# A windowed-attention phase ahead of two expert layers: its instructions ordered by a list scheduler inside the kernel, with all PSUM banks in one pool

## The chip, the cores and the metric

One core of one Trainium2 chip runs the kernel. The engines are TensorE (PE, with its weight loads shown as PEld), VectorE (DVE), ScalarE (ACT), GpSimd (POOL) and the queue that issues most transfers (SP). The metric is the device time of one execution in microseconds (us).

## What is computed

Four batches of eight heads (512 local and 32 global tokens, 64 channels each) go through attention, and the result goes through two dense layers one after the other:

```python
s_g = scale * np.matmul(q_g, k_all.transpose(0, 1, 3, 2))
out_g = np.matmul(sm(s_g), v_all)
...
mask = np.abs(pos[:, None] - pos[None, :]) <= window
...
a_l = sm(s_l)
out_l = np.matmul(a_l, np.concatenate([v_g, v_l], axis=2))
...
return (silu * val @ w_out).astype(np.float32)
...
return (g @ w_out).astype(np.float32)
```

Local queries see the keys within 32 positions and the 32 global keys; global queries see all 544 keys. The first dense layer (512 to 1536 to 512) gates with silu, the second (512 to 2048 to 512) is a mish layer.

## The kernel before

**Two phases.** The first phase is the attention, in function `attention()` (L342). The second phase, from L644 on, holds the dense layers; it is emitted inside `tc.manual_schedule()`, that is, in the order written. The 2176 rows of x are cut in five column tiles of 512, 384, 384, 384 and 512 (`TILES`), x0 to x4; each value is kept as a high and a low part (x0h, x0l), and every dense product is three matmuls (high by high, high by low, low by high).

**A pair.** The attention works on pairs of heads: 4 batches of 4 pairs, 16 in all. `att_hp` (L197) takes one pair through its steps, each ended by a `yield`: turn queries and keys with 16 transposes (L195, tile qkT), copy them to SBUF (keys on DVE L211, queries on ACT L215, more keys on POOL L212 and L213); twice, for two halves, scores (L238, tile sc), masked minimum on DVE (L243) and exponential on ACT (L247); normalise on POOL (L228, L230); turn the weights (L195, tile pT) and copy them (ACT L265); multiply by the values (L272 and L276, tile o); split into x high (ACT L137) and x low (DVE L138). `att_g` (L281) does the same for the global queries of two pairs at once (tiles ga, gT, go), 8 times. `att_glob` (L325) prepares the global keys and queries of a batch.

**Fills.** The first group of the first dense layer is done early for x0, x1 and x2: `fill` (L524) emits, per tile, four accumulations of 12 matmuls (g and v, L538, for two slices of 128 hidden channels) and four of 6 (L559). They need x of a whole batch and the first six weight pieces. The weights are packed as doubles and are unpacked by `w_convert` (L399): a square on ACT (L407), four DVE operations (L409 to L413), a copy on ACT (L423) and a subtraction on POOL (L424).

**What sets the order.** `attention()` writes the steps down with hand-set times (pair n at 10n, converts at 16 to 48, fills at a priority of a million below), sorts them, and emits them in that order. The framework's scheduler then orders each engine's instructions itself, by priority and a timeline simulated at compile time (`schedule_with_timeline_sim=True`, L692). In the compiled program the steps of pairs, converts and fills stand interleaved.

**Buffers.** PSUM has 8 banks of 512 words per partition: three pairs of banks for the attention (`ps_pair`, `bank()` L143) and two single banks for the fills (`ps_mm`). Keys, queries, values and scores of a pair are double-buffered. SP issues the loads: six per pair for queries and keys (L162 to L166), four for values (L185 to L187), one per weight piece (L393, L396).

Of the kernel before, what the change touches and what calls it, by code (L numbers as in the profile page):

```python
# [21 lines left out]
def tile_attn_moe_moe2(  # L22
# [109 lines left out]
    def split_to_x(src, kd, nk, c0, n):  # L132
        for t, o, s, m in pieces(c0, n):
            xh, xl = x_tile(t)
            hi = xh[:, kd:kd + nk, o:o + m]
            lo = xl[:, kd:kd + nk, o:o + m]
            nc.scalar.activation(out=hi, in_=src[:, :, s:s + m], func=AF.Copy)  # L137
            nc.vector.tensor_tensor(out=lo, in0=src[:, :, s:s + m], in1=hi.bitcast(F32), op=ALU.subtract)  # L138
# [4 lines left out]
    def bank(name):  # L143

        return ps_pair.tile([128, 2, 512], F32, tag="pair", name=name)
# [3 lines left out]
    def load_glob(b):  # L149
        gk = g_p.tile([128, 2, 128], F32, tag="gkq", name="gkq")  # L150
        for i, src in enumerate((k_g, q_g)):
            for h in range(2):
                (nc.sync if b else nc.scalar).dma_start(out=gk[:, i, 64 * h:64 * h + 64],
                                  in_=src[b].rearrange("(g h) p d -> h g p d", h=2)[h])
        GK[b] = gk

    def load_qk(b, hp):
        hs = slice(2 * hp, 2 * hp + 2)
        qs = qk_p.tile([128, 4, 2, D], F32, tag="qs", name="qs")
        ks = qk_p.tile([128, 4, 2, D], F32, tag="ks", name="ks")  # L160
        for h in range(2):
            nc.sync.dma_start(out=ks[:, :, h], in_=k_l[b, 2 * hp + h].rearrange("(c p) d -> p c d", p=128))  # L162
            nc.sync.dma_start(out=qs[:, 0:3, h],
                              in_=q_l[b, 2 * hp + h, SG:SG + 384, :].rearrange("(c p) d -> p c d", p=128))
        nc.sync.dma_start(out=qs[0:96, 3], in_=q_l[b, hs, SG + 384:SL, :].rearrange("h p d -> p h d"))
        nc.sync.dma_start(out=qs[96:128, 3], in_=q_l[b, hs, 0:SG, :].rearrange("h p d -> p h d"))  # L166
        QS[b, hp], KS[b, hp] = qs, ks
# [29 lines left out]
    def att_hp(b, hp):  # L197


        qs, ks = QS.pop((b, hp)), KS.pop((b, hp))  # L200
        p = bank("qkT")
        for i, src in enumerate((ks, qs)):
            for r in range(4):
                for j in range(2):
                    transpose_half(p[:, j, 256 * i + 64 * r:256 * i + 64 * r + 64],
                                   src[half(j), r].rearrange("p h d -> p (h d)"), j)
        pk, pq = (p[:, :, 256 * i:256 * i + 256].rearrange("c j (r t) -> c r j t", t=64) for i in range(2))
        kst = kst_p.tile([128, 4, 224], F32, tag="kst", name="kst")
        KST[b, hp] = kst
        nc.gpsimd.tensor_copy(kst[:, :, 192:224], GK[b, "kT"][:, hp:hp + 1, :].to_broadcast([128, 4, SG]))  # L210
        nc.vector.tensor_copy(kst[:, :, 0:128].rearrange("c r (j t) -> c r j t", j=2), pk)  # L211
        nc.gpsimd.tensor_copy(kst[:, 0:3, 128:192], kst[:, 1:4, 0:64])  # L212
        nc.gpsimd.tensor_copy(kst[:, 3, 128:192], kst[:, 0, 0:64])  # L213
        qT = qk_p.tile([128, 4, 128], F32, tag="qT", name="qT")
        nc.scalar.activation(out=qT.rearrange("c r (j t) -> c r j t", j=2), in_=pq, func=AF.Copy)  # L215
        yield
        sm = sm_p.tile([128, NB, 224], F32, tag="sm", name="sm")
        sng = sm_p.tile([128, NB, SG], F32, tag="sng", name="sng")
        nb_ = st_p.tile([128, NB], F32, tag="nb", name="nb")
        su = st_p.tile([128, NB], F32, tag="su", name="su")  # L220
        rc = st_p.tile([128, NB], F32, tag="rc", name="rc")

        def normalise(g):
            i0, i1 = 4 * g, 4 * g + 4
            r = rc[:, i0:i1]
            nc.vector.tensor_scalar(r, su[:, i0:i1], 1e-9, None, op0=ALU.add)
            nc.vector.reciprocal(r, r)  # L227
            nc.gpsimd.tensor_tensor(out=sm[:, i0:i1, 0:192], in0=sm[:, i0:i1, 0:192],  # L228
                                    in1=r.unsqueeze(2).to_broadcast([128, 4, 192]), op=ALU.mult)
            nc.gpsimd.tensor_tensor(out=sng[:, i0:i1, :], in0=sm[:, i0:i1, 192:224],  # L230
                                    in1=r.unsqueeze(2).to_broadcast([128, 4, SG]), op=ALU.mult)


        for g in range(2):
            p = bank("sc")
            for pp in range(2):
                for h in range(2):
                    nc.tensor.matmul(p[:, h, 224 * pp:224 * pp + 224], lhsT=qT[half(h), 2 * g + pp, :],  # L238
                                     rhs=kst[half(h), 2 * g + pp, :], start=True, stop=True)
            for pp in range(2):  # L240
                for h in range(2):
                    i = 4 * g + 2 * pp + h
                    nc.vector.tensor_tensor_reduce(  # L243
                        out=sm[:, i], in0=p[:, h, 224 * pp:224 * pp + 224],
                        in1=mask7 if 2 * g + pp == 3 else mask, scale=-scale, scalar=3.0e38,
                        op0=ALU.add, op1=ALU.min, accum_out=nb_[:, i:i + 1])
                    nc.scalar.activation(out=sm[:, i], in_=sm[:, i], func=AF.Exp,  # L247
                                         bias=nb_[:, i:i + 1], scale=-1.0, accum_out=su[:, i:i + 1])
            if g:
                normalise(0)  # L250
            yield
        normalise(1)
        yield


        pt = []
        for g in range(2):
            p = bank("pT")
            for k in range(4):
                for j in range(2):  # L260
                    transpose_half(p[:, j, 64 * k:64 * k + 64], sm[half(j), 4 * g + k, 64 * j:64 * j + 128], j)
            for j in range(2):
                transpose_half(p[:, j, 256:320], sng[half(j), 4 * g:4 * g + 4].rearrange("q b x -> q (b x)"), j)
            pt.append(sm_p.tile([128, 2, 5, 64], F32, tag=f"pt{g}", bufs=1, name="pt"))
            nc.scalar.activation(out=pt[g].rearrange("k j x q -> k j (x q)"), in_=p[:, :, 0:320], func=AF.Copy)  # L265
            yield
        vw = VW[b, hp]
        p = bank("o")[:, 0]
        for r in range(4):
            for h in range(2):  # L270
                k = 2 * (r % 2) + h
                nc.tensor.matmul(p[half(h), 128 * r:128 * r + 128], lhsT=vg[:, k, hp, :],  # L272
                                 rhs=pt[r // 2][:, :, 4, :], start=(r == 0), stop=False)
        for i in range(NB):
            for h in range(2):
                nc.tensor.matmul(p[half(h), 64 * i:64 * i + 64], lhsT=vw[:, i, h, :],  # L276
                                 rhs=pt[i // 4][:, i % 2, 2 * (i // 2 % 2) + h, :], start=False, stop=(i == NB - 1))
# [418 lines left out]
```

## Time and profile before

| what | value |
|---|---|
| median of 3 runs | 1004.9 us (1004.61 to 1005.93) |
| profiled execution, its own time | 1006.5 us |
| span of that execution in the profile | 1004.8 us |
| PE busy over the span | 944.4 us (94%) |
| PE granted clock, mean | 0.973 of full speed |
| DVE, ACT, POOL busy | 571.8, 523.8, 362.0 us |

Times in the rows count from the start of the span. Busy time is time in which an engine has an instruction in flight; matmuls overlap one another, so the step from one group's start to the next group's start is shorter than the listed duration of a group. PEclk is the granted TensorE clock as a share of 2.4 GHz; 0.5 is the lower of its two levels. In the chain of waits each row is what held up the end at that moment.

### The profile page before, as it was taken

Reading aid. Unit: us, or ns where it says so; the run is one execution under the profiler, and the core shown is the slowest. Engines: PE = TensorE matmul, PEld = TensorE weight load, DVE = VectorE, ACT = ScalarE, POOL = GpSimd, SP = SyncE. Lnnn points to the kernel's source line nnn. Section 1 sums busy time; section 2 is a strip of 40 time slices with the busy share of each in tenths; the row PEclk is TensorE's granted clock in tenths of the full one; section 3 lists DMA queues with packets and bytes.
Section 4 is the critical chain, followed back from the end, with each engine's and each line's share of the span. In section 5 each row is a group of like instructions: output and inputs, shape, how many; then the busy total and the mean of one; then the engine's idle time right before and its main releaser. Section 6 shows DMA issues by size and latency. Waiting matters only on the chain.

```text
span 1004.8 us, 15751 instructions
## 1 busy us (share of the span) xinstructions
PE 944.4 (94%) x6008; PEld 822.3 (82%) x6008; DVE 571.8 (57%) x1097; ACT 523.8 (52%) x1058; POOL 362.0 (36%) x353
## 2 busy tenths in 40 slices
PE   5588987988999999999999999999999999999998
PEld 4366776767899899898898998898889789888986
DVE  3855554454888765846838745556444826562213
ACT  3456565554233222312223335788668867886664
POOL 3443343432443432323323454543234423342222
PEclk9688999987999999999999999999999999999999
DMA  6643343410222211201202101021102101100112
GB/s 141 192 109 75 90 93 85 94 43 22 78 70 84 63 64 36 69 22 42 76 10 63 63 1 43 22 63 43 42 22 64 63 22 42 43 22 1 59 47 73
DMA packets 101387, 59.21 MB, mean 59 GB/s; under 512 B 75072, under 2 KB 95552, under 8 KB 101312
## 3 DMA queue, kind: packets, MB, share of 16 engines
q1 hardware_dynamic: 100784, 58.08, 20.8%
q8 instruction: 47, 0.77, 0.3%
q14 instruction: 28, 0.23, 0.1%
q10 hardware_dynamic: 528, 0.13, 0.1%
HBM read 53.74 MB, written 4.46 MB: 58 GB/s over the span
## 4 chain that ended last, share of the span: by engine, by line
PE 80%; DVE 9%; ACT 7%; POOL 1%; issue 1%; DMA 1%; SPq 0%; DVEq 0%; ACTq 0%; POOLq 0%
PE acc L603 29%; PE h L447 16%; PE v L447 13%; PE g L447 13%; ACT sm L247 4%; PE sc L238 2%; DVE cx L412 1%; PE mm L559 1%; POOL sm L228 1%; PE g L538 1%; DVE fl L409 1%; PE v L538 1%; DVE sm L243 1%; PE pT L195 1%; DVE cx L411 1%
## 5 line engine op out<-in xcount | busy, mean ns | idle before, releaser
L458 POOL TENSOR_TENSOR al<-t,ah 128x384 fp32r<-128x384 f32 (+1 forms) x140 | 164.1, 1187 | 462.0 <-ACT ah L472 451.0
L472 ACT ACTIVATE ah<-t 128x384 fp32r<-128x384 f32 (+1 forms) x140 | 79.2, 566 | 147.2 <-DVE t L483 132.9
L512 DVE TENSOR_TENSOR t<-t,h 128x384 f32<-128x384 f32 (+1 forms) x80 | 47.1, 607 | 142.5 <-ACT t L511 142.3
L611 DVE TENSOR_TENSOR y<-acc,y 128x512 f32<-128x512 f32 (+1 forms) x151 | 92.6, 636 | 43.2 <-PE acc L603 42.5
L480 ACT ACTIVATE t<-g 128x384 f32<-128x384 f32 (+1 forms) x54 | 28.9, 536 | 134.0 <-PE g L447 133.0
L412 DVE SCALAR_TENSOR_TENSOR cx<-fl,cx 128x512 uint32<-128x512 uint32 x68 | 81.6, 1200 | 2.2
L228 POOL TENSOR_TENSOR sm<-sm,rc 128x768 f32<-128x768 f32 x32 | 47.5, 1484 | 91.3 <-DVE rc L227 78.6
L247 ACT ACTIVATE sm<-sm,nb 128x224 f32<-128x224 f32 x128 | 60.1, 471 | 35.6 <-DVE nb L243 35.5
L501 ACT ACTIVATE t<-h 128x384 f32<-128x384 f32 (+1 forms) x80 | 41.9, 523 | 58.3 <-PE h L447 58.2
L413 DVE SCALAR_TENSOR_TENSOR cx<-st,cx 128x512 uint32<-128x512 uint32 x68 | 67.2, 988 | 2.3
L481 DVE SCALAR_TENSOR_TENSOR t<-t,g 128x384 f32<-128x384 f32 (+1 forms) x54 | 32.7, 606 | 56.7 <-ACT t L480 56.6
L409 DVE SCALAR_TENSOR_TENSOR fl<-q,st 128x512 f32<-128x512 f32 x68 | 59.5, 875 | 9.6 <-ACT q L407 9.6
L483 DVE SCALAR_TENSOR_TENSOR t<-t,v 128x384 f32<-128x384 f32 (+1 forms) x54 | 32.9, 609 | 46.9 <-PE v L447 46.0
L243 DVE CUSTOM_DVE_ANT_0 sm<-sc,mask 128x224 f32<-128x224 f32 x128 | 42.2, 385 | 28.2 <-PE sc L238 28.2
L502 ACT ACTIVATE t<-t,cst 128x384 f32<-128x384 f32 (+1 forms) x80 | 52.8, 660 | 2.6
L511 ACT ACTIVATE t<-t,cst 128x384 f32<-128x384 f32 (+1 forms) x80 | 49.4, 649 | 0.3
L407 ACT ACTIVATE q<-st 128x512 f32<-128x512 f32 x68 | 44.6, 656 | 7.7 <-DMA st<-in_moe_w_gate 4.4
L411 DVE TENSOR_SCALAR cx<-fl 128x512 uint32<-128x512 uint32 x68 | 43.8, 644 | 5.6
L238 PE MATMUL sc<-kst,qT 64*128 64x224 f32 x256 | 38.7, 426 | 2.8 <-ACT qT L215 2.0
L511 ACT ACT_TABLE_LOAD x27 | 34.6, 1283 | 0.5
L500 ACT ACT_TABLE_LOAD x27 | 34.6, 1283 | 0.5
L195 PE MATMUL pT<-ident,sm 64*128 64x64 f32 x256 | 16.2, 252 | 18.9 <-POOL sm L228 18.3
(899 smaller groups left out, 2812.8 us busy)
## 6 DMA issues: line engine op xcount, KB each, us to landing
st<-in_moe_w_out SPq DMA_DIRECT2D x28, 512.0 KB
st<-in_moe_w_in SPq DMA_DIRECT2D x16, 512.0 KB
vw<-in_v_l SPq DMA_DIRECT2D x32, 224.0 KB
st<-in_moe_w_gate SPq DMA_DIRECT2D x12, 512.0 KB
st<-in_moe_w_val SPq DMA_DIRECT2D x12, 512.0 KB
ks<-in_k_l SPq DMA_DIRECT2D x32, 128.0 KB
qs<-in_q_l SPq DMA_DIRECT2D x32, 96.0 KB
out<-y SPq DMA_DIRECT2D x12, 256.0 KB
```

The lines of the kernel that those rows point to most:

```text
L228: nc.gpsimd.tensor_tensor(out=sm[:, i0:i1, 0:192], in0=sm[:, i0:i1, 0:192], in1=r.unsqueeze(2).to_broadcast([128, 4, 192]), op=ALU.mult)
L238: nc.tensor.matmul(p[:, h, 224 * pp:224 * pp + 224], lhsT=qT[half(h), 2 * g + pp, :], rhs=kst[half(h), 2 * g + pp, :], start=True, stop=True)
L247: nc.scalar.activation(out=sm[:, i], in_=sm[:, i], func=AF.Exp, bias=nb_[:, i:i + 1], scale=-1.0, accum_out=su[:, i:i + 1])
L409: nc.vector.scalar_tensor_tensor(fl, q, TINY2, hw, op0=ALU.is_ge, op1=ALU.mult)
L412: nc.vector.scalar_tensor_tensor(x, fu, 0xC0000000, x, op0=ALU.bitwise_and, op1=ALU.bitwise_or)
L413: nc.vector.scalar_tensor_tensor(x, st[:, :, 0], 29, x, op0=ALU.logical_shift_right, op1=ALU.bitwise_or)
L447: nc.tensor.matmul(p[:, 0:n], lhsT=a[:, d], rhs=c[:, k, :], start=(k == 0 and j == 0), stop=(k == KD - 1 and j == 2))
L458: nc.gpsimd.tensor_tensor(out=a[1][:, 0:n], in0=src, in1=a[0][:, 0:n].bitcast(F32), op=ALU.subtract)
L472: nc.scalar.activation(out=a[0][:, 0:n], in_=src, func=AF.Copy)
L511: nc.scalar.activation(out=s, in_=s, func=AF.Sin, scale=-2.0, bias=quarter)
L603: nc.tensor.matmul(p, lhsT=l, rhs=r, start=(first and j == 0), stop=(last and j == 2))
L611: nc.vector.tensor_tensor(out=ya, in0=p, in1=ya, op=ALU.add)
```

## The change

Each step of the attention, of the six weight conversions and of the three fills becomes a task: a name, a key (its nominal time), an engine, a duration, the tasks that it needs, the work that it emits, and the PSUM banks that it takes with the task that frees them. `in_order()` runs a list scheduler over the tasks while the kernel is built: whenever an engine is free it takes the task of lowest key whose needs are done and whose banks are free. The tasks are emitted in that order, now inside `tc.manual_schedule()`, so that each engine runs them as planned.

With it: the 8 PSUM banks are four fixed tiles of two banks, from which a task takes a pair (`both`) or one bank (`one`); the second phase gets its own `ps_mm` after the attention, and its PSUM pools wait tile by tile. A fill is cut into portions of three matmuls with keys above 1000. The conversions have keys from 35 on, 5 apart, and their four DVE operations are tasks of their own. The copy of the queries goes to ACT for even pairs and to DVE for odd ones. The scores of global queries against global keys (L289, two matmuls for each two pairs) are made once per batch in one bank (`GG`) and copied to SBUF. The loads are tasks of SP; the queries of pair 0 are issued from the ACT queue, and the first global keys and queries from SP instead of ACT.

The core of the diff (the work functions emit the instructions of before and are left out):

```diff
-    ps_mm = pool("ps_mm", 2, space=PS)
...
-    ps_pair = pool("ps_pair", 3, early, space=PS)
+    ps_pair = pool("ps_pair", 1, early, space=PS)
...
+    PAIR = [ps_pair.tile([128, 2, 512], F32, tag=f"pair{i}", name=f"pair{i}") for i in range(4)]
...
+    def both(task):
+        return PAIR[place[task][0] // 2]
+
+    def one(task):
+        i = place[task][0]
+        return PAIR[i // 2][:, i % 2]
...
+        eng = nc.sync if b or hp else nc.scalar
...
+        done, start, order = {}, {}, []
+        used = [None] * 8
+        free = {"PE": 0.0, "DVE": 2.0, "ACT": 2.5, "POOL": 3.0, "SP": 0.0}
+        wait = {e: sorted((n for n in tasks if tasks[n][1] == e), key=lambda n: tasks[n][0]) for e in free}
+        now = 0.0
+        while any(wait.values()):
+            for i in range(8):
+                if used[i] is not None and done.get(used[i], 1e9) <= now:
+                    used[i] = None
+            for e, queue in wait.items():
+                if free[e] > now:
+                    continue
+                for n in queue:
+                    key, _, room, needs, work, banks, until = tasks[n]
+                    if any(done.get(x, 1e9) > now for x in needs):
+                        continue
+                    if banks == 2:
+                        got = next(([2 * i, 2 * i + 1] for i in range(4) if used[2 * i] is used[2 * i + 1] is None), None)
+                    elif banks == 1:
+                        some = [i for i in range(8) if used[i] is None]
+                        got = [min(some, key=lambda i: used[i ^ 1] is None)] if some else None
+                    else:
+                        got = []
+                    if got is None:
+                        continue
+                    for i in got:
+                        used[i] = until
+                    place[n] = got
+                    late = {"PE": 0.25, "SP": 2.4}.get(e, 0.08)
+                    if n[0] == "w":
+                        late = 4.5
+                    free[e] = now + room
+                    done[n] = now + room + late
+                    order.append(n)
+                    queue.remove(n)
+                    break
+            later = [x for x in list(free.values()) + list(done.values()) if x > now]
+            if not later:
+                raise RuntimeError("no task can start: " + str({e: q[:3] for e, q in wait.items()}))
+            now = min(later)
+        return order
...
+        task(("A", n), t - 4, "PE", 0.65, [("qk", n)], qk, 2, ("Aq", n))
+        task(("Ag", n), t - 3.95, "POOL", 0.30, [("AGk", b), lastu("GA", n - 2), agog("S", 2, 1)], glob_keys)
+        task(("Ak", n), t - 3.9, "DVE", 0.69, [("A", n), lastu("GA", n - 2), agog("S", 2, 1)], keys)
+        task(("At", n), t - 3.8, "POOL", 0.55, [("Ak", n)], more_keys)
+        task(("Aq", n), t - 3.7, "ACT" if on_act else "DVE", 0.60 if on_act else 0.69,
+             [("A", n), ("Ak", n), agog("S", 2, 1)], queries)
...
+            task(("S", n, g), t + 0.5 * g, "PE", 0.98, [("Aq", n), ("At", n), ("Ag", n)], lambda g=g: scores(g), 2, ("M", n, g, 3))
+            for i in range(4):
+                task(("M", n, g, i), t + 0.5 * g + 0.1 * i, "DVE", 0.31,
+                     [("S", n, g), agog("C", 2, 1)], lambda g=g, i=i: minimum(g, i))
+                task(("E", n, g, i), t + 0.5 * g + 0.1 * i, "ACT", 0.49, [("M", n, g, i)], lambda g=g, i=i: exponential(g, i))
+            task(("R", n, g), t + 1 + g, "DVE", 0.38, [("E", n, g, 3)], lambda g=g: reciprocal(g))
+            task(("N", n, g), t + 1 + g, "POOL", 1.9, [("R", n, g), agog("C", 2, g)], lambda g=g: normalise(g))
+            task(("C", n, g), t + 2 + g, "PE", 0.42, [("N", n, g)], lambda g=g: turn(g), 2, ("V", n, g))
+            task(("V", n, g), t + 2 + g, "ACT", 0.70, [("C", n, g), ago("D", 1)], lambda g=g: turned(g))
...
+        task(("D", n), t + 4, "PE", 2.05, [("V", n, 0), ("V", n, 1), ("v", n), ("vg", b)], values, 1, ("Xl", n))
+        task(("Xh", n), t + 4, "ACT", 0.82 if b else 0.65, [("D", n)], lambda: x_high(src(), hp, 1, b * SL, SL))
+        task(("Xl", n), t + 4, "DVE", 0.90 if b else 0.70, [("Xh", n)], lambda: x_low(src(), hp, 1, b * SL, SL))
+        task(("qk", n), t - 24, "SP", 3.1 if n else 1.6, [ago("A", 2)], lambda: load_qk(b, hp))
+        task(("v", n), t - 12, "SP", 2.1, [ago("D", 2), lastu("GO", n - 2)], lambda: load_v(b, hp))
...
+        task(("GA", u), t, "PE", 0.95, [("Ak", n), ("Ak", n - 1), ("AGe", b)], scores, 1, ("GE", u))
+        task(("GM", u), t, "DVE", 1.1, [("GA", u), ("GGe", b)], minimum)
+        task(("GE", u), t, "ACT", 1.2, [("GM", u), ago("GT")], exponential)
+        task(("GR", u), t + 1, "DVE", 0.9, [("GE", u)], normalise)
+        task(("GT", u), t + 1, "PE", 0.40, [("GR", u)], turn, 2, ("GV", u))
+        task(("GV", u), t + 2, "ACT", 0.70, [("GT", u), ago("GO")], turned)
+        task(("GO", u), t + 3, "PE", 1.25, [("GV", u), ("v", n), ("v", n - 1), ("vgb", b)], values, 1, ("GXl", u))
...
+        task(("AGe", b), t + 3, "DVE", 0.6, [("AG", b, 1), ("AGk", b)] + prev(("GA", HP // 2 * b - 1), ("GG", b - 1)), queries)
+        task(("GG", b), t + 3, "PE", 0.3, [("AGe", b)], scores, 1, ("GGe", b))
+        task(("GGe", b), t + 3, "DVE", 0.2, [("GG", b)] + prev(("GE", HP // 2 * b - 1)), scored)
...
+        task(("Cq", i), t, "ACT", 0.67, [("w", i)] + ([("Cf", i - 1, 0)] if i else []), go)
+        for j, room in enumerate((0.7, 0.45, 0.68, 0.68)):
+            need = [("Cf", i, j - 1)] if j else [("Cq", i)] + ([("Cf", i - 1, 3), ("Cl", i - 2)][:i] if i else [])
+            task(("Cf", i, j), t + 0.1 * j, "DVE", room, need, go)
+        task(("Ch", i), t, "ACT", 0.63, [("Cf", i, 3)], go)
+        task(("Cl", i), t, "POOL", 1.3, [("Ch", i)], go)
...
+            add_pair(n)
+        for i in range(9):
+            task(("w", i), CT(i) - 10.0, "SP", 0.6, [("Cf", i - 3, 3)] if i > 2 else [], load_next)
+        for i in range(6):
+            add_convert(i)
+        for i in FILL:
+            add_fill(i)
+        for name in in_order():
+            tasks[name][4]()
...
+                    need = x_done + [("Cl", piece), before if c else None]
+                    task(("F", t, f, kind, c), key, "PE", 0.012 + n * 0.00142, need,
+                         lambda k=k, f=f, kind=kind, c=c: unit(k, f, kind, c),
+                         0 if c else 1, ("Fg" if kind == "g" else "Fp", t, f))
...
+                task(("F2", t, c, i), key, "PE", 0.012 + n * 0.00142, need, lambda c=c, i=i: second_part(c, i),
...
-    attention()
+    with tc.manual_schedule():
+        setup()
+        attention()
     early.close()
-    ps_acc = pool("ps_acc", 4, space=PS)
-    ps_at = pool("ps_at", 2, space=PS)
+    ps_acc = pool("ps_acc", 4, space=PS, reuse_waits="tile")
+    ps_mm = pool("ps_mm", 2, space=PS, reuse_waits="tile")
+    ps_at = pool("ps_at", 2, space=PS, reuse_waits="tile")
```

Names of tasks: A turns queries and keys; Ag, Ak, At, Aq copy them; S scores; M minimum; E exponential; R reciprocal; N normalise; C turns the weights; V copies them; D multiplies by the values; Xh and Xl split; GA to GX the same for global queries; AG, GG the preparations of a batch; Cq to Cl a conversion; F and F2 the portions of a fill.

## Rows read from the trace of the kernel before

**Rows 1.** The page, part 1: busy time, share of the span, instructions.

```profile
PE 944.4 (94%) x6008; PEld 822.3 (82%) x6008; DVE 571.8 (57%) x1097; ACT 523.8 (52%) x1058; POOL 362.0 (36%) x353
```

**Rows 2.** Busy time by stretch: stretch, length, then engines, PEclk, DMA share, GB/s.

```profile
0.00:241.30 241.30, 189.35 (x2301) 149.48 (x2301) 127.07 (x486) 131.77 (x407) 89.41 (x137) 0.89 0.40 96
241.30:1004.80 763.50, 755.08 (x3708) 672.84 (x3708) 444.77 (x612) 392.05 (x651) 272.57 (x216) 1.00 0.15 47
```

**Rows 3.** The same view for six stretches of the first phase.

```profile
5.60:27.00 21.40, 15.28 (x138) 12.07 (x140) 7.00 (x35) 8.16 (x28) 7.23 (x13) 1.00 0.66 148
27.00:60.00 33.00, 19.77 (x194) 15.02 (x192) 27.52 (x65) 18.78 (x49) 15.29 (x16) 0.64 0.69 196
60.00:100.00 40.00, 34.09 (x415) 25.54 (x416) 20.74 (x87) 23.14 (x75) 15.63 (x23) 0.91 0.31 69
100.00:160.00 60.00, 56.09 (x754) 46.02 (x755) 32.62 (x136) 36.22 (x115) 22.45 (x34) 1.00 0.42 96
160.00:206.00 46.00, 37.47 (x452) 29.97 (x450) 24.51 (x105) 26.21 (x86) 17.73 (x27) 0.93 0.32 73
206.00:241.30 35.30, 26.62 (x357) 20.82 (x353) 13.02 (x59) 17.98 (x56) 8.82 (x14) 0.76 0.14 32
```

**Rows 4.** The chain of waits, first 50 us: start, duration, what.

```profile
3.53 2.03 DMA qs<-in_q_l
...
8.96 0.61 ACT qT L215
...
24.93 3.73 DMA st<-in_moe_w_gate
...
44.37 1.96 DVE fl L409
```

**Rows 5.** PE in order of time: start, duration, group [idle before].

```profile
78.82 1.10 PE L276 MATMUL o<-pt,vw 128*64 128x64 f32 x32
...
237.20 1.92 PE L276 MATMUL o<-pt,vw 128*64 128x64 f32 x32
...
241.27 0.41 PE L447 MATMUL v<-x3h,w1h 128*128 128x384 f32 x1 [0.62 <-DVE x4l L138]
```

**Rows 6.** PE in order of time at full clock, 198 to 213 us.

```profile
198.21 1.03 PE L286 MATMUL ga<-kst,qgbd 128*64 128x512 f32 x4
...
199.25 1.03 PE L238 MATMUL sc<-kst,qT 64*128 64x224 f32 x8
...
203.13 0.33 PE L559 MATMUL mm<-ah,w5h 128*128 128x384 f32 x1
...
203.65 0.33 PE L559 MATMUL mm<-ah,w4h 128*128 128x384 f32 x1
...
204.78 0.53 PE L195 MATMUL gT<-ident,sg 64*128 64x64 f32 x10
205.14 0.42 PE L195 MATMUL qkT<-ident,ks 64*128 64x64 f32 x8
...
205.65 0.41 PE L195 MATMUL pT<-ident,sm 64*128 64x64 f32 x8
...
206.05 0.44 PE L447 MATMUL g<-x3h,w0h 128*128 128x384 f32 x1
...
206.78 0.66 PE L320 MATMUL go<-gtl,vw 128*64 128x32 f32 x16
...
208.06 0.46 PE L195 MATMUL pT<-ident,sm 64*128 64x64 f32 x8
...
209.33 1.09 PE L272 MATMUL o<-pt,vg 128*64 128x128 f32 x16
...
211.29 1.03 PE L238 MATMUL sc<-kst,qT 64*128 64x224 f32 x8
212.15 0.41 PE L195 MATMUL qkT<-ident,ks 64*128 64x64 f32 x8
```

**Rows 7.** PE, one group of scores in the last stretch.

```profile
218.44 1.81 PE L238 MATMUL sc<-kst,qT 64*128 64x224 f32 x8
```

More of the change, by code (lines that the diff above doesn't have):

```diff
@@ L1 @@
-import itertools
 from contextlib import ExitStack
@@ new lines, in tile_attn_moe_moe2, with task, in_order @@
+    tasks = {}
+    QACT = lambda n: n % 2 == 0
+    CT = lambda i: 35.0 + 5 * i
+    def task(name, key, engine, room, needs, work, banks=0, until=None):
+        tasks[name] = (key, engine, room, [x for x in needs if x is not None], work, banks, until)
+    def in_order():
+        done, start, order = {}, {}, []
[39 more added lines that the diff above has]
+        return order
@@ L231, in normalise @@
                                     in1=r.unsqueeze(2).to_broadcast([128, 4, SG]), op=ALU.mult)
[L234 to L258, printed above, removed]
+        def turn(g):
+            p = both(("C", n, g))
             for k in range(4):
                 for j in range(2):
-                    transpose_half(p[:, j, 64 * k:64 * k + 64], sm[half(j), 4 * g + k, 64 * j:64 * j + 128], j)
+                    transpose_half(p[:, j, 64 * k:64 * k + 64], R["sm"][half(j), 4 * g + k, 64 * j:64 * j + 128], j)
             for j in range(2):
[L263 to L266, printed above, removed]
@@ L565, in low_priority @@
-    def low_priority(t):
-        p = tc.cur_priority
-        tc.cur_priority = p + 1000000
-        for _ in fill(t):
-            pass
-        tc.cur_priority = p
+                    slow = [("Fl", t, fs[k - 1])] if k else [("Fl", t - 1, fs[1])] if t else []
+                    task(("Ft", t, f), key, "ACT", 0.57, [before] + slow, lambda f=f: gate(f))
+                    task(("Fg", t, f), key, "DVE", 0.65, [("Ft", t, f)], lambda f=f: gated(f))
+                else:
+                    task(("Fp", t, f), key, "DVE", 0.65, [before, ("Fg", t, f)], lambda f=f: product(f))
+                    task(("Fh", t, f), key, "ACT", 0.60, [("Fp", t, f)] + ([("F2", t - 1, KD - 1, 1)] if t else []),
+                         lambda f=f: a_high(f))
+                    task(("Fl", t, f), key, "POOL", 1.2, [("Fh", t, f)], lambda f=f: a_low(R["a", f], R["s", f], n))
@@ L572, in out_rows @@
+        for c in range(KD):
+            for i in range(2):
+                need = [before if i else None, ("Fl", t, fs[0]), ("Fl", t, fs[1]), ("Cl", 4), ("Cl", 5)]
+                task(("F2", t, c, i), key, "PE", 0.012 + n * 0.00142, need, lambda c=c, i=i: second_part(c, i),
+                     0 if i else 1, ("Fy", t, c))
+                before = ("F2", t, c, i)
+                key += 1
+            task(("Fy", t, c), key, "DVE", 0.69, [before], lambda c=c: copy(c))
     def out_rows(c0, n):
```

440 lines of the change are left out of this document (250 added, 190 removed).

## The prediction

> **What bounds the kernel now.** I read part 1 of the page first: PE is busy for 94% of the span, far ahead of the others [rows 1]. So PE's time is the time, and the question is where the remaining 6% lies. Busy time by stretch answers it [rows 2]. From 241.3 us on PE is busy for 755.1 of 763.5 us at full clock, and the change leaves that part's work and order alone. Before 241.3 us it is busy for 189.4 of 241.3 us, at a mean clock of 0.89: 52 us idle, and many of the busy ones slow. No other engine fills that phase either (ACT 131.8, DVE 127.1, POOL 89.4 us). So the first phase is bound by order: engines wait for each other by turns.
>
> Six stretches show where [rows 3]. The worst is 27 to 60 us: PE busy 19.8 of 33 us at clock 0.64, with DVE busy 27.5 us. The chain of waits says what DVE does there: it waits for a weight piece that lands at 28.7 us, and then runs the conversions ahead of the attention [rows 4]. The fourth pair's last matmuls start only at 78.8 us; the sixteenth pair's at 237.2 us, 12 pairs later, which is 13.2 us a pair [rows 5]. The best stretch, 100 to 160 us, has PE busy 56.1 of 60 us at full clock; the last has 26.6 of 35.3 us at clock 0.76, and its group of scores takes 1.81 us where one at full clock lists 1.03 [rows 3, 6, 7].
>
> **What the first phase needs of PE.** The steps from start to start at full clock give each task's price [rows 6]: A 0.51 us (205.14 to 205.65), S 0.86 (211.29 to 212.15), C 0.40 (205.65 to 206.05), D 1.96 (209.33 to 211.29); for two pairs' global queries GA 1.04 at most (198.21 to 199.25, with the two small matmuls that the change moves to `GG`), GT 0.36, GO 1.28 (206.78 to 208.06); a fill portion of three matmuls of 384 columns 0.52 (203.13 to 203.65), of 512 columns by proportion 0.69.
> - Pairs: 0.51 + 2 x 0.86 + 2 x 0.40 + 1.96 = 4.99, times 16 = 79.8 us.
> - Global queries: 2.68 x 8 = 21.4 us.
> - Fills: 24 portions a tile (16 F, 8 F2): 2 x 24 x 0.52 + 24 x 0.69 = 41.5 us.
> - Preparations of a batch: no row of their own in the list; I take one S each, 3.4 us (between 0 and twice that).
> Sum 146 us, against the 239.1 us that the phase takes now: the second phase's first v product starts at 241.27 us [rows 5], and the g product ahead of it, spread over the last 35 us, is four portions of 0.52 = 2.1 us.
>
> **The change, part by part.**
> - *Order.* The plan runs on durations like those of the rows (S 0.98, D 2.05, A 0.65 against 0.86, 1.96, 0.51), so that it is somewhat slower than PE can be. Three matmuls of a fill are the most that stands ahead of a ready attention task on PE (0.5 to 0.7 us).
> - *The start.* The first transposes wait for queries that land at 5.56 us; the first query copy ends at 9.6 us [rows 4]. The issue of queries moves to the ACT queue and that of the global keys to SP; each is a few issues earlier or later, and I take 0 (bounds: 2 us either way, the 2.03 us of that load).
> - *Batch 0.* No fill can run before it. Now its end is at about 82 us (78.8 us and the split). With conversions behind the attention by key, the pace is ACT's: 131.8 us over 16 pairs, all its work counted, is 8.2 us a pair, so 4 x 8.2 = 33 us from 9.6 us, and about 7 us from the last exponential to x (N, C, V, D, Xh, Xl; the last pair of before goes from its last 32 matmuls to the next phase in 4.1 us [rows 5], and I put 3 us to the steps ahead). Batch 0 ends near 50 us. PE has by then done 4 x 4.99 + 2 x 2.68 = 25 us and about 5 us of pairs 4 and 5. What hides the conversions then is DVE's slack beside ACT; without it their DVE work adds 15 us here (by the plan's durations 0.70 + 0.45 + 0.68 + 0.68 = 2.51 us, six times).
> - *The rest.* 146 - 30 = 116 us of PE work, with a fill portion ready for nearly every gap. At the busy share of the best stretch, 0.93, this takes 125 us; at 1.0, 116; at the share of the last stretch, 0.75, 155 [rows 3]. I take 0.93, as that stretch is nearest to it: attention and fills mixed. ACT needs 12 x 8.2 = 98 us in this time, so PE is last.
> - *Banks.* Four pairs of banks shared by all replace three and two singles. A fill holds two or three singles, so the attention has two or three pairs at such times, as now; costed at 0, with the wait for a bank inside the 0.93.
> - *SP.* Ten loads a pair and one per weight piece, some 5 us of issue a pair against 8 us of pace. A load that waits for its buffer holds up the loads behind it; the plan knows this. The loads of 27 to 60 us ran at 196 GB/s [rows 3], and batch 0 needs some 9 MB by my count (half a MB each: keys with queries of six pairs, values of five, seven weight pieces): 46 us, just under the 50. Costed at 0, bound +5.
> - *Query copies to DVE* (8 of 0.6 us) and *four copies of `GG`*: beside PE, no cost while DVE has slack.
> - *Second phase.* The same instructions. Its banks may come free sooner; at most the 4.1 us between the last pair and its first v product is shared [rows 5]. Costed at 0.
>
> **Sum.** The second phase's PE work starts at 50 + 125 = 175 us instead of 239.1: 64 us less. Against the profiled execution's 1006.5 us that is 942; it stands 1.6 us above the median of the runs, so I predict 941 us. Bounds: 165 us with no gap in the rest, less 5 for a faster start, gives 926; 205 us, the share of 0.75, gives 971.
>
> **A cold first batch.** In 27 to 60 us, PE was busy for 60% and the granted clock was 0.64, mixing its two levels; in 5.6 to 27 us it was busy for 71% at 1.00 [rows 3]. At the lower level attention without fills costs PE twice 6.3 us a pair, more than ACT's 8.2: batch 0 would end at 9.6 + 4 x 12.6 + 7 = 67 us, and the whole at 941 + 17 = 958. With PE at 6.3 of 8.2 us (77%) the first of the two stretches is the nearer, so I give this 0.10. The Trainium skill's page "TensorE: Matmul & The Clock Gate" (section "Part 1: The HAM clock gate") says that the throttled state is the default and that activity releases it; by that rule alone a batch without fills is in danger and the sum would be 958. The stretch of 5.6 to 27 us does not bear it out as a danger at such a share.
>
> **The rivals.**
> - *Stretched rounds* (0.16): the fixed order makes each small lateness a wait for all engines, and pairs keep near their pace of 13.2 us, say 11.5: 50 + 12 x 11.5 + 7 = 195 us, 961. For it: even the best stretch took about 12 us a pair. Against: PE was full there.
> - *Late loads* (0.06): the plan allows 2.4 us after an issue and 4.5 for a weight piece; the rows show 2.03 and 3.73, early on [rows 4]. If each pair waits 3 us more, 48 us come back: 989.
> - *Banks that wait for their twin* (0.05), the slower side: the pairs are four fixed tiles. If a matmul into one half waits until the reader of the other half is done, each of some 64 single-bank uses (16 D, 16 GA and GO, 24 accumulations of fills, 8 of batches) waits about one D, 1.96 us: 125 us, 1066. It decides from 1.0 us each (64 us over 64). Nothing in the trace shows it, as before uses separate tiles.
> - *The order is not obeyed* (0.02): the context still has its simulated timeline; then it stays within 2 us of 1005. Against: the second phase is written in the same way and runs PE at 99%.
>
> **How the numbers follow.** The forecast has 0.61, the cold batch 0.10, the stretched rounds 0.16: all faster, with late loads 0.93 in all. What a measurement of this kernel cannot tell from no change is 0.2%, 2 us: 0.02. Slower 0.05. The range goes from 926 to 970, which takes in the forecast's bounds, the cold batch and the stretched rounds, and leaves out late loads and both rest cases.
>
> **What would show it.** In the changed profile: the fourth pair's last L276-like matmuls near 45 us instead of 78.8; PE's busy share 0.9 or more from 50 us to the start of the second phase, with clock 1.00; the first matmul of the second phase near 175 us, and from there 763 us as now. PE idle before scores, released by DVE or ACT, would mean stretched rounds; idle engines released by DMA, late loads; PE idle before single-bank tasks, released by a reader of another task, the twin banks. If the second phase is itself longer, the sum is wrong at its root.

## The result and the profile after

The change makes the kernel faster: 965.2 us (median of 4 runs, 964.1 to 966.1) against 1005.4 beside it, a ratio of 0.960 (95%: 0.958 to 0.962). That is 40 us where 64 were forecast. 965 lies inside the range of 926 to 970, but 24 us above the forecast itself; it is inside because the range takes in the rivals as well. The profiled execution takes 964.1 us with a span of 962.4.

Part 1 of the page after answers to [rows 1]: busy time, share of the span, instructions.

```profile
PE 927.0 (96%) x6008; PEld 811.5 (84%) x6008; DVE 580.2 (60%) x1109; ACT 518.4 (54%) x1050; POOL 362.7 (38%) x353
```

Busy time by stretch after, in the columns of [rows 2], split where the second phase's first matmul starts; then stretches as in [rows 3], the last of them running into the second phase.

```profile
0.00:196.90 196.90, 169.91 (x2289) 136.66 (x2289) 135.00 (x496) 125.88 (x398) 90.38 (x137) 0.95 0.50 118
196.90:962.40 765.50, 757.11 (x3721) 674.85 (x3720) 445.16 (x614) 392.50 (x652) 272.35 (x216) 1.00 0.15 47
...
5.60:27.00 21.40, 17.66 (x232) 13.23 (x230) 13.41 (x55) 13.03 (x43) 8.46 (x17) 0.92 0.69 157
27.00:60.00 33.00, 28.31 (x388) 21.68 (x384) 27.69 (x96) 22.92 (x74) 16.22 (x24) 0.90 0.72 178
60.00:100.00 40.00, 32.05 (x488) 26.14 (x488) 32.83 (x108) 29.52 (x89) 23.61 (x28) 0.91 0.66 164
100.00:160.00 60.00, 57.99 (x784) 44.73 (x782) 42.81 (x169) 42.35 (x140) 30.47 (x47) 1.00 0.42 95
160.00:206.00 46.00, 42.14 (x456) 38.94 (x452) 22.42 (x76) 18.85 (x58) 10.54 (x11) 0.96 0.11 25
```

The second phase is what it was: 765.5 us from its first matmul on, against 1004.8 - 239.1 = 765.7. So all of the gain lies in the first phase, and 27 to 60 us shows it best: PE busy 28.3 of 33 us at clock 0.90, where it was 19.8 at 0.64 [rows 3]. From 100 to 160 us PE is full, 97% at clock 1.00.

The clock column of these views needs care at the start. The trace holds its first record of the clock at 25.3 us before and at 11.1 us after, and up to there the view prints 1.00. The durations say otherwise. PE before: eight transposes and a group of scores in front of the first record, and a group of scores behind it.

```profile
18.92 0.69 PE L195 MATMUL pT<-ident,sm 64*128 64x64 f32 x8 [1.90 <-POOL sm L228]
19.40 1.80 PE L238 MATMUL sc<-kst,qT 64*128 64x224 f32 x8
...
26.53 1.03 PE L238 MATMUL sc<-kst,qT 64*128 64x224 f32 x8
```

PE after, eight transposes on either side of the first record:

```profile
4.74 0.69 PE L203 MATMUL pair<-ident,ks 64*128 64x64 f32 x8 [4.74 <-DMA ks<-in_k_l]
...
11.31 0.41 PE L203 MATMUL pair<-ident,ks 64*128 64x64 f32 x8
```

1.80 us is the lower level, as the 1.81 of [rows 7]. So 5.6 to 27 us, which the prediction read as full clock [rows 3], ran at the lower level up to 25.3 us; the 0.92 of that stretch after is too high as well.

PE in order of time after: the last matmuls of pairs 4 and 16, as in [rows 5], the first fill portion, the hole behind batch 0, and the second phase's first matmul.

```profile
49.22 1.10 PE L380 MATMUL pair<-pt,vw 128*64 128x64 f32 x32
53.88 0.48 PE L705 MATMUL pair<-x0h,w0h 128*128 128x512 f32 x1
...
63.53 0.47 PE L203 MATMUL pair<-ident,sm 64*128 64x64 f32 x8 [3.15 <-DVE nb L323]
66.19 0.69 PE L203 MATMUL pair<-ident,sm 64*128 64x64 f32 x8 [2.12 <-ACT pt L358]
68.03 1.97 PE L376 MATMUL pair<-pt,vg 128*64 128x128 f32 x16
...
179.59 1.10 PE L380 MATMUL pair<-pt,vw 128*64 128x64 f32 x32
...
196.90 0.33 PE L617 MATMUL g<-x3h,w0h 128*128 128x384 f32 x1
```

Pair 4 ends 30 us earlier than before, pair 16 ends 58 us earlier, at (179.59 - 49.22) / 12 = 10.9 us a pair instead of 13.2. Part of that is paid back: the fills that the order has put off run behind the attention, and the phase itself is shorter by 42 us.

To compare with the forecast I split PE's time up to the second phase into three, from busy time in the stretches between two changes of the clock, with the stretch in front of the first record at the lower level: **work**, busy time times granted clock (PE's load at full clock); **low clock**, the rest of the busy time; **idle**.

| up to the second phase's first matmul | work | low clock | idle | sum |
|---|---|---|---|---|
| before (with 2.1 us of second-phase work) | 160.9 | 28.4 | 52.0 | 241.3 |
| after | 157.4 | 12.5 | 27.0 | 196.9 |
| forecast | 146 | 29, with idle | | 175 |

The 42 us come from idle time (25) and low clock (16); PE's work stays within 2 us. The miss of 22 us is 11 of work and 11 of low clock and idle time.

### The profile page after: what moved, and what is told of

Read it like the earlier page. It is cut to its first block, busy times and chain, and to the rows that moved or that the text cites. A ratio compares the mean times of both kernels' runs of the same rounds, so it can differ in the third digit from the quotient of the medians.

```text
span 962.4 us, 15775 instructions
## 1 busy us (share of the span) xinstructions
PE 927.0 (96%) x6008; PEld 811.5 (84%) x6008; DVE 580.2 (60%) x1109; ACT 518.4 (54%) x1050; POOL 362.7 (38%) x353
## 4 chain that ended last, share of the span: by engine, by line
PE 86%; DVE 5%; ACT 4%; issue 1%; DMA 1%; SPq 1%; POOL 1%; DVEq 0%; ACTq 0%; POOLq 0%
PE acc L802 30%; PE h L617 17%; PE g L617 13%; PE v L617 13%; PE pair L705 4%; PE pair L312 2%; PE pair L203 2%; PE pair L376 2%; PE pair L380 1%; DVE cx L576 1%; PE pair L449 1%; DVE fl L574 1%; ACT sm L330 1%; DVE cx L575 1%; PE pair L405 1%
## 5 line engine op out<-in xcount | busy, mean ns | idle before, releaser
L650 ACT ACTIVATE t<-g 128x384 f32<-128x384 f32 (+1 forms) x54 | 28.9, 535 | 143.0 <-PE g L617 142.0
L671 ACT ACTIVATE t<-h 128x384 f32<-128x384 f32 (+1 forms) x80 | 41.8, 523 | 58.3 <-PE h L617 58.2
L651 DVE SCALAR_TENSOR_TENSOR t<-t,g 128x384 f32<-128x384 f32 (+1 forms) x54 | 32.7, 606 | 59.1 <-ACT t L650 59.0
L323 DVE CUSTOM_DVE_ANT_0 sm<-pair,mask 128x224 f32<-128x224 f32 x128 | 42.7, 385 | 6.1 <-PE pair L312 6.0
L312 PE MATMUL pair<-kst,qT 64*128 64x224 f32 x256 | 32.8, 385 | 1.3 <-ACT pt L358 0.9
L312 PEld LDWEIGHTS pair<-kst,qT 64*128 64x128 f32 x256 | 23.4, 195 | 5.9 <-issue 1.5
```

The costliest lines, as they stand in the source:

```text
L312: nc.tensor.matmul(p[:, h, 224 * pp:224 * pp + 224], lhsT=R["qT"][half(h), 2 * g + pp, :], rhs=KST[b, hp][half(h), 2 * g + pp, :], start=T ...
```

## The experiments

Ratios are against the kernel before, run on the same chip; phase 2 is when the second phase's first matmul starts.

| run | us | ratio (95%) | phase 2 | work / low clock / idle |
|---|---|---|---|---|
| the change | 965.2 | 0.958–0.962 | 196.9 | 157.4 / 12.5 / 27.0 |
| w_late | 986.6 | 0.979–0.982 | 217.2 | 159.9 / 21.9 / 35.4 |
| sp_true | 964.7 | 0.958–0.961 | 195.4 | 161.4 / 9.1 / 24.9 |
| banks_split | 977.5 | 0.971–0.975 | 210.1 | 161.3 / 16.7 / 32.1 |
| conv_early | 981.4 | 0.975–0.978 | 215.0 | 159.3 / 15.6 / 40.1 |
| fill_coarse4 | 973.8 | 0.966–0.970 | 203.8 | 157.1 / 8.3 / 38.4 |
| no_fills | 979.7 | 0.972–0.975 | 168.5 | 111.6 / 15.9 / 40.9 |
| fills_two | 963.3 | 0.955–0.959 | 182.1 | 143.5 / 9.6 / 28.9 |
| pe_switch | 969.4 | 0.962–0.966 | 201.9 | 159.0 / 9.8 / 33.1 |
| conv_light | 961.6 | 0.953–0.958 | 193.8 | 157.7 / 11.1 / 25.0 |
| w_reuse | 965.1 | 0.957–0.962 | 196.4 | 157.2 / 11.6 / 27.5 |
| both_light | 961.4 | 0.954–0.958 | 193.2 | 157.7 / 11.4 / 24.0 |
| late_more | 963.0 | 0.955–0.960 | 194.2 | 160.0 / 7.7 / 26.4 |

**Does the plan's idea of the loads cost the time?** Two runs give the scheduler later loads.

w_late:
```
-                        late = 4.5
+                        late = 12.0
```


> The scheduler is told that a weight piece needs 12 us after its issue instead of 4.5; nothing else changes. Theory 1 (late loads): from 48 us on the pairs fall behind because ACT stands in front of the squares of the pieces until they land (2.9 us at 57 to 60 us) and the exponentials queue behind it. Then the second phase starts some 5 us sooner than 197 us, total 960 or less. Theory 2 (slow engines: DVE operations next to POOL and PE at its lower clock take longer than planned): the loads don't matter, and the conversions placed later only delay the fills, total 965 to 970.

Measured 986.6, 21 us worse and outside both theories. PE in order of time: pair 4, pair 5 and the first fill portion.

```profile
49.16 1.10 PE L380 MATMUL pair<-pt,vw 128*64 128x64 f32 x32
62.79 1.92 PE L380 MATMUL pair<-pt,vw 128*64 128x64 f32 x32
68.80 0.79 PE L705 MATMUL pair<-x0h,w0h 128*128 128x512 f32 x1
```

Batch 0 ends as before this edit and pair 5 is 7 us earlier (69.79 with the change), but the scheduler, told that pieces land late, puts the conversions late; the fills start at 68.8 instead of 53.9 us. What the fills lose at the start is not made good.

sp_true:
```
-                    late = {"PE": 0.25, "SP": 2.4}.get(e, 0.08)
+                    late = {"PE": 0.25, "SP": 3.5}.get(e, 0.08)
...
-        task(("qk", n), t - 24, "SP", 3.1 if n else 1.6, [ago("A", 2)], lambda: load_qk(b, hp))
-        task(("v", n), t - 12, "SP", 2.1, [ago("D", 2), lastu("GO", n - 2)], lambda: load_v(b, hp))
+        task(("qk", n), t - 24, "SP", 4.6 if n else 1.6, [ago("A", 2)], lambda: load_qk(b, hp))
+        task(("v", n), t - 12, "SP", 2.9, [ago("D", 2), lastu("GO", n - 2)], lambda: load_v(b, hp))
```


> The scheduler is told the load costs that the trace of the changed kernel shows on SP: 4.6 us of issue for queries and keys, 2.9 for values, 3.5 us to landing (instead of 3.1, 2.1, 2.4). Theory 1 (late loads): the order fits what happens, second phase some 4 us or more sooner, total 961 or less. Theory 2 (slow engines): 965 within 2.

Measured 964.7, no difference. The figures were taken from the trace after: SP in order of time, the same two issues of queries in a pair of 33 us and in the next one.

```profile
33.55 0.98 SPq L171 DMA_DIRECT2D qs<-in_q_l  x2
...
41.04 3.24 SPq L171 DMA_DIRECT2D qs<-in_q_l  x2
```

With the larger figures no engine waits for a transfer between 20 and 100 us any more, and still the total is the same: idle time and low clock fall by 2 and 3 us, PE's work rises by 4. So late loads were there, but are not what holds the phase.

**Two parts undone, with the scheduler left in place.** banks_split keeps fills to two banks of their own, and leaves three pairs to the attention:
```
-                        got = next(([2 * i, 2 * i + 1] for i in range(4) if used[2 * i] is used[2 * i + 1] is None), None)
+                        got = next(([2 * i, 2 * i + 1] for i in range(3) if used[2 * i] is used[2 * i + 1] is None), None)
...
-                        some = [i for i in range(8) if used[i] is None]
+                        some = [i for i in (range(6, 8) if n[0] in ("F", "F2") else range(6)) if used[i] is None]
```


> Undoes the shared pool: the attention takes banks from three pairs only, the fills from the fourth, as before the change. If banks are worth nothing, as the forecast costed them: 965 within 3. If the shared pool carries part of the gain: the attention or the fills wait for banks, second phase 8 us or more later, total 973 or more.

Measured 977.5: with this plan the pool is worth 12 of the 40 us. From 100 to 160 us PE falls from 57.99 busy us to 54.90, and its clock from 1.00 to 0.92.

```profile
100.00:160.00 60.00, 54.90 (x732) 42.78 (x733) 37.19 (x159) 37.86 (x128) 24.65 (x40) 0.92 0.41 93
```

conv_early puts the conversions ahead by key, near where the kernel before had them, and the loads of their pieces early:
```
-    CT = lambda i: 35.0 + 5 * i
+    CT = lambda i: 16.0 + 6 * i
...
-            task(("w", i), CT(i) - 10.0, "SP", 0.6, [("Cf", i - 3, 3)] if i > 2 else [], load_next)
+            task(("w", i), 9.0, "SP", 0.6, [("Cf", i - 3, 3)] if i > 2 else [], load_next)
```


> Puts the conversions back to the times of before (keys 16 to 46, 6 apart, their loads at 9). The forecast's reading, that the conversions ahead of the attention made the worst stretch: batch 0 is complete later than now (first fill portion after 60 us instead of 56), total 970 to 975. Rival: the list scheduler fits them in wherever they stand, total 965 within 2.

Measured 981.4, worse than both expectations: the place of the conversions and of their loads is worth 16 us; no run moves one without the other. PE in order of time: pairs 2, 3 and 4 and the longest wait between them.

```profile
30.02 1.10 PE L380 MATMUL pair<-pt,vw 128*64 128x64 f32 x32
47.79 0.45 PE L471 MATMUL pair<-ident,gkq 128*128 128x128 f32 x1 [7.02 <-DMA gkq<-in_k_g]
52.81 1.92 PE L380 MATMUL pair<-pt,vw 128*64 128x64 f32 x32
62.72 1.92 PE L380 MATMUL pair<-pt,vw 128*64 128x64 f32 x32
```

Here a late transfer does hold PE, for 7 us: its issue stands in SP's order at 44.71 us, among the loads of later pairs. Batch 0 ends 13.5 us later and the fills start at 84 us.

**What is PE's load made of?** fill_coarse4 makes a fill task of 12 matmuls instead of 3 (`STEP = 4` blocks of 128 rows in one task, planned at four times the time):
```
+    STEP = 4
...
-                for c in range(KD):
+                for c in range(0, KD, STEP):
...
-                    task(("F", t, f, kind, c), key, "PE", 0.012 + n * 0.00142, need,
+                    task(("F", t, f, kind, c), key, "PE", STEP * (0.012 + n * 0.00142), need,
```


> The g and v portions of the fills are twelve matmuls instead of three; the same matmuls in all. Theory 3 (price of a change of kind): a portion that follows its own kind takes 0.52 us and one between attention tasks 0.72 to 0.76, so the first phase holds some 160 changes of 0.1 us that the forecast's 146 us left out; with fewer changes PE's busy time times clock up to the second phase falls by some 4 us. The total then is 961 if the longer blocks ahead of attention tasks cost nothing. Rival (waits): the blocks of 2.1 to 2.8 us delay the attention, and the total is 967 or more although the work falls.

Measured 973.8: the idle time grows by 11 us, and the work stays (157.1 against 157.4). The edit hardly takes changes of kind away: in the trace the fills stand in 26 unbroken stretches after and in 23 here, as the order already puts portions together. So this run does not test their price. What it shows is that blocks of up to 2 us, some 3 for the tile of 512 columns, delay the whole; that it is the attention's DVE and ACT steps behind them that come late is the expectation's reading, not shown apart.

no_fills and fills_two take fills out of the first phase; the second phase does that work instead:
```
-    FILL = [0, 1, 2]
+    FILL = []
```
and in fills_two
```
+    FILL = [0, 1]
```


> No fills in the attention phase: the first group of the first layer is done for all five tiles in the second phase. Theory 3: the attention alone needs some 112 us of PE, so ACT's 8.2 us a pair bounds it and the second phase starts near 150 to 155 us; the moved work costs 42 us there without changes of kind, total 957 to 962. Rival (waits between engines bound the attention, as in the stretched rounds): the second phase starts at 170 us or later, total 975 or more.

> Only the fills of the first two tiles stay in the attention phase; the third, which in the changed kernel runs mostly alone after the attention and ends with PE idle 2.5 us and at its lower clock, goes to the second phase. Theory 3: its 12.5 us run there without waits, second phase some 16 us earlier and 12.5 us longer, total 961 or less. Rival: the third fill covers waits of the last pairs, and the total is 965 or more.

no_fills: 979.7 us, the second phase starts at 168.5. Attention alone needs 111.6 us of PE's work, where the forecast's terms without the fills make 104.6, and it runs at 168.5 / 16 = 10.5 us a pair, start and end included (9.9 from pair 4 to pair 16), not at ACT's 8.2. Busy time from 100 to 160 us:

```profile
100.00:160.00 60.00, 48.53 (x856) 38.74 (x853) 43.27 (x199) 49.11 (x174) 30.82 (x47) 0.96 0.49 111
```

No engine is full here, ACT as the busiest at 82%: without fills the pairs are held by engines that wait for each other. Since the fills take 45.8 us of work (157.4 - 111.6) and push the second phase by only 28.4 (196.9 - 168.5), 17.4 us of them lie in time that was idle or lost to the low clock, near the 14.5 us by which the whole is shorter with them. fills_two: 963.3, its interval overlaps the change's; the third tile's fills earn nothing that can be measured.

pe_switch gives the scheduler PE's durations as measured start to start, and 0.1 us more for every task:
```
-                    free[e] = now + room
-                    done[n] = now + room + late
+                    free[e] = now + room + (0.1 if e == "PE" else 0.0)
+                    done[n] = free[e] + late
...
-        task(("A", n), t - 4, "PE", 0.65, [("qk", n)], qk, 2, ("Aq", n))
+        task(("A", n), t - 4, "PE", 0.51, [("qk", n)], qk, 2, ("Aq", n))
```
and in the same way S 0.87 for 0.98, D 1.96 for 2.05, and a fill portion `n * 0.00135` for `0.012 + n * 0.00142`.

> The scheduler gets PE durations from the rows of before (0.51, 0.87, 1.96, 0.52) and adds 0.1 us for each task, as a price of the change of kind. Theory 3: the plan comes closer to what the chip does, but PE's work stays, so 963 to 966. Rival (wrong durations make the waits): total 960 or less.

Measured 969.4, 4 us worse, outside both expectations. Batch 0 ends sooner (pair 4 at 44.9 us), but the fills start at 70.6: this order gives the time back.

**What holds the phase between 50 and 70 us?** The chip's pairs fall behind the order's own plan, by 5.6 us at pair 4 and 10.7 at pair 5 (59.1 planned, 69.8 on the chip). Two causes were taken away one by one and together. conv_light leaves out three of the four DVE operations of the six early conversions; w_reuse leaves out the loads of pieces 3 to 5; both_light joins the two edits.
```
+        if fine:
+            steps = [lambda: None,
+                     lambda: nc.vector.tensor_scalar(x, st[:, :, 1], 3, 0x3FFFFFFF, op0=ALU.logical_shift_left, op1=ALU.bitwise_and),
+                     lambda: None, lambda: None]
```


> Order and loads as in the changed kernel; of the four DVE operations of each of the six early conversions only one is left (12 us of DVE less between 42 and 82 us; the weights of these pieces are not the right ones). Theory 2 (DVE runs the conversions longer than planned, up to 1.65 us where 0.68 are planned, and the pairs stand behind): the fifth pair's last matmuls start at 63 us or before instead of 69.8, second phase 6 us or more sooner, total 959 or less. Theory 1 (late weight pieces stop ACT): 963 to 966.

```
+        i = order.index(p)
+        if 3 <= i < 6:
+            STG[p] = KEPT[i - 3]
+            return
```


> Order as in the changed kernel; the loads of weight pieces 3, 4 and 5 are left out, and their conversions read pieces 0, 1 and 2 again (1.5 MB and three issues less between 56 and 69 us). Theory 1 (late loads): ACT's waits of 2.9 and 0.8 us in front of the squares go, second phase 4 us or more sooner, total 961 or less. Theory 2: 963 to 966.

> Both of the edits before in one kernel, order unchanged. If DVE's conversions and late pieces cover for each other (each alone gains little, as the other is late as well), both together gain 8 us or more, total 957 or less; if the lateness comes from neither (waits between engines, changes of kind on PE), 962 to 966.

conv_light 961.6, w_reuse 965.1, both 961.4. Pair 5 ends at 66.7, 69.2 and 63.6 us instead of 69.8. So the conversions cost some 3.5 us (the two intervals just touch) and the three loads nothing that can be measured; with both gone pair 5 is 6 us earlier and the whole still only 3.8 us shorter.

The plan knows nothing of the clock, and the trace of the change shows what that leaves out. Busy time after in the stretches at the lower level, the first at 1.00 only because nothing is on record there:

```profile
0.00:11.10 11.10, 5.54 (x40) 4.16 (x42) 4.63 (x16) 2.96 (x7) 3.30 (x17) 1.00 0.66 150
17.90:21.30 3.40, 3.40 (x40) 2.86 (x38) 2.20 (x12) 2.41 (x9) 0.00 (x0) 0.50 0.72 160
38.40:41.80 3.40, 3.13 (x41) 2.88 (x39) 1.91 (x5) 2.90 (x10) 2.59 (x7) 0.50 0.89 239
55.40:58.80 3.40, 3.40 (x26) 2.04 (x23) 3.37 (x10) 1.77 (x8) 3.08 (x3) 0.51 0.58 149
65.70:72.50 6.80, 6.31 (x80) 5.58 (x82) 6.66 (x19) 4.75 (x14) 4.72 (x4) 0.50 0.87 231
```

Half of PE's busy time there is lost: 6.0 us up to pair 4 and 9.5 up to pair 5, near the 5.6 and 10.7 by which they are late. This is an account of the time; no run sets the clock.

late_more makes every task of the plan last longer, so that the order leans less on exact times:
```
-                    late = {"PE": 0.25, "SP": 2.4}.get(e, 0.08)
+                    late = {"PE": 0.35, "SP": 2.4}.get(e, 0.2)
```


> The scheduler allows 0.35 us instead of 0.25 from PE's end to the next engine and 0.2 instead of 0.08 from the others. If the many short waits between engines, longer than planned, make the pairs late: total 960 or less. If the lateness has one early cause (loads or conversions): 965 within 3.

Measured 963.0, and its interval overlaps the change's. Of the runs that compute everything, none is clearly better than the change.

## Why the prediction was right, and where its size was off

- **What bounds it: right.** PE, by idle time and low clock in the first phase; the second phase is untouched. The gain is 41 of 42 us from just these two.
- **"What the first phase needs of PE": the step that failed.** Sum 146 us, measured 157.4: 11 of the 22 us missing are here. Counting each group after from its start to the next group's start, without idle time and at the clock of its stretch, the attention takes 109.6 us where the sum has 104.6, and the fills 47.7 where it has 41.5. D and GO cost what the forecast took; A 0.64 instead of 0.51, S 0.90 instead of 0.86, C 0.45 instead of 0.40. Two things are missing in the prices. The price of a fill portion, and that of A, comes from a row among its own kind; next to another kind a task costs more. PE in order of time after, a portion of 384 columns among its own kind (186.97 to 187.49: 0.52) and one among transposes (150.17 to 150.89: 0.72), and a matmul behind idle time:

```profile
186.97 0.33 PE L705 MATMUL pair<-x2h,w2h 128*128 128x384 f32 x1
187.15 0.33 PE L705 MATMUL pair<-x2l,w2h 128*128 128x384 f32 x1
187.32 0.33 PE L705 MATMUL pair<-x2h,w2l 128*128 128x384 f32 x1
187.49 0.33 PE L705 MATMUL pair<-x2h,w3h 128*128 128x384 f32 x1
...
150.02 0.23 PE L203 MATMUL pair<-ident,sng 64*128 64x64 f32 x2
150.17 0.44 PE L705 MATMUL pair<-x1h,w3h 128*128 128x384 f32 x1
150.45 0.34 PE L705 MATMUL pair<-x1l,w3h 128*128 128x384 f32 x1
150.63 0.33 PE L705 MATMUL pair<-x1h,w3l 128*128 128x384 f32 x1
150.89 0.46 PE L203 MATMUL pair<-ident,ks 64*128 64x64 f32 x8
...
190.54 0.45 PE L705 MATMUL pair<-ah,w5h 128*128 128x384 f32 x1 [1.33 <-ACT ah L642]
```

  The matmul behind a change lists 0.44 instead of 0.33 us, as does one behind idle time among its own kind: 0.1 us at each end of a stretch of fills, and with 26 such stretches some 5 of the fills' 6 us. The other thing is PE's stops. A price from start to start holds only where the next group follows at once; where PE stops, the last matmul counts with its full listed time. It does so behind 28 attention groups, for 5.6 us more than the usual steps, as much as the attention is over its sum. No run takes either away, so the two sizes are read from the trace and not shown by an edit. The sum could have been had from rows of before: PE's work there was 158.8 us (160.9 less the 2.1), and the durations written into the plan add up to 156.
- **Batch 0: about right.** The first fill portion starts at 53.9 us, forecast 50; pair 4's last matmuls at 49.2, forecast near 45. The 8.2 us a pair of ACT was not the pace, though: pairs 1 to 4 follow each other at 9.6 us (20.4 to 49.2), which makes the 4 us, and without fills pairs 4 to 16 at 9.9.
- **"The rest", 0.93 at full clock: near as a mean, not in its course.** From the first fill portion to the second phase PE is busy for 129.2 of 143 us, 0.90, at clock 0.95. From 100 to 160 us it is better (97%, clock 1.00), from 60 to 100 us worse (32.05 of 40 us at 0.91). There PE idles 3.15 and 2.12 us behind DVE and ACT, and right behind this the first half of D takes 1.97 us where 1.09 is its time at full clock.
- **Conversions in DVE's slack: partly.** They were costed at nothing, 15 us as their plain DVE work. Taking most of it away gives some 3.5 us. DVE in order of time after, the last step of the third conversion and of the fifth, and POOL at the third:

```profile
60.39 1.65 DVE L577 SCALAR_TENSOR_TENSOR cx<-st,cx 128x512 uint32<-128x512 uint32 x1
...
74.12 0.68 DVE L577 SCALAR_TENSOR_TENSOR cx<-st,cx 128x512 uint32<-128x512 uint32 x1
```

```profile
59.73 1.76 POOL L341 TENSOR_TENSOR sm<-sm,rc 128x768 f32<-128x768 f32 x1 [0.38 <-DVE rc L336]
61.45 0.84 POOL L343 TENSOR_TENSOR sng<-sm,rc 128x128 f32<-128x128 f32 x1
```

  The operation lasts 1.65 us while POOL normalises, against a median of 0.69 over its six. The Trainium skill, page "SBUF — State Buffer", section "Who interferes with whom", says that a DVE instruction with two SBUF inputs contends with a GpSimd instruction that reads SBUF, since the second input comes through the read interface that they share. The row at 60.39 us agrees; at 74.12 us the same operation keeps its 0.68 us beside two copies of keys on POOL, so not every overlap costs time.
- **Banks at 0: wrong, in the change's favour.** Banks of their own for the fills cost 12 us (banks_split).
- **SP at 0, bound 5: right for the total, wrong in detail.** Waits for weight pieces are small in the change; the waits of after list 2.8 us on ACT's square of one piece:

```profile
ACT q L571 <- DMA st<-in_moe_w_val: 2.8, 1, 2.8
```

- **The rivals.** *Stretched rounds* named 961, nearer than the forecast, with 11.5 us a pair and 10.9 measured. Its mechanism holds for attention alone (no_fills: 9.9 us a pair with no engine full) and between 50 and 70 us; from 100 to 160 us PE is full, which it does not have. *Late loads*: present and small, except where the order makes them large (conv_early). *The cold batch* did not come as a whole: of batch 0's time, 0 to 11.1, 17.9 to 21.3 and 38.4 to 41.8 us are at the lower level, which costs 12.5 us in the whole phase. But the forecast held it unlikely for a wrong reason: it set 5.6 to 27 us, 71% busy, against it as a stretch at full clock, and that stretch ran at the lower level up to 25.3 us, so it does not speak against the rule that the prediction cites either. That the clock rose sooner here, at 11.1 us, was luck for the forecast. *The twin banks* aren't there: they need 64 us of waiting before they decide, and PE idles for 27.0 us in the whole phase. *The order not obeyed* is refuted by the time, 965 where it has 1005.
- **What the plan leaves out, and what stays open.** The order's own plan ends PE's first-phase tasks at 181.5 us, later than the forecast's 175, and the chip needs 196.9. By the split above these 15 us are low clock (12.5), work (157.4 against the plan's 156.1) and idle time (27.0 against 25.4). The conversions explain 3.5; true load times (sp_true) and true PE times (pe_switch) changed the order without making the chip faster. What would keep the clock up was not tried. Nor were the query copies on DVE and the four `GG` taken out, nor the need of a whole batch before a fill: in the kernel before a first fill matmul starts at 33.75 us, when only the first pair is through, while the plan lets a portion start only when all four are.

## What to carry to other kernels

Price the tasks of a mixed order from a stretch where they are mixed, or take the whole phase's busy time times its clock; prices from a run of one kind, and from places where PE does not stop, are a lower bound (here 146 against 157 us). Check a clock of 1.00 at the start of a trace against the durations of one kind of matmul. A list schedule gains by filling idle time, and needs small filler tasks and free banks for it (9 and 12 us here). Its order is touchy: other figures for loads or PE gave 0, 21 and 4 us worse, so each set of figures has to be timed, and the plan's own end, which the code can tell, is an optimistic bound worth reading first: it has no clock.

## What the runs showed of the hardware that was not expected

- A matmul behind one of another kind, or behind idle time, lists 0.44 instead of 0.33 us (384 columns), and a portion between other kinds takes 0.72 from start to start instead of 0.52.
- Up to the first record of the clock (25.3 us before, 11.1 after) the view prints 1.00, while eight transposes take 0.69 us instead of 0.41.
- Issuing two transfers took SP 0.98 us at 33.55 us and 3.24 us at 41.04, in a stretch that moved 178 GB/s.
- One conversion step on DVE took 1.65 us instead of 0.69 beside a normalisation on POOL, and 0.68 beside two copies.
